# Gram products in eight row and column groups of TensorE, two batches at a time

## The chip, the cores and the metric

The kernel runs on one NeuronCore of a Trainium2 chip. The metric is device time in microseconds of one execution, the median over the runs shown. A profile page and a trace come from one more execution, which has a time of its own.

## What is computed

Inputs are q, k, v of shape (4 batches, 8 heads, 768 positions, 48) and beta of shape (4, 8, 768), with the weights of two layers that follow. The reference runs a delta rule per batch and head, and then two dense layers with a nonlinearity each:

```python
k_n = k / (np.linalg.norm(k, axis=-1, keepdims=True) + 1e-06)
for t in range(S):
    y[:, :, t] = np.einsum('bhd,bhde->bhe', q[:, :, t], state)
    v_old = np.einsum('bhde,bhd->bhe', state, kt)
    state = state + bt[:, :, :, None] * np.einsum('bhd,bhe->bhde', kt, vt - v_old)
# x: y as (3072 tokens, 384)
h = x @ w_in          # 384 -> 2048
g = np.where(h > 0.0, h, np.exp(np.minimum(h, 0.0)) - 1.0)
x = g @ w_out         # 2048 -> 384
# second layer: the same shapes, g = P(h) / Q(h), a cubic over a quadratic in |h|
```

All inputs are float32. The result is the second layer's output, 3072 x 384.

## The kernel before

**The delta rule by chunks.** The 768 positions are cut into 12 segments `s` of 64, and each segment of a head into two blocks of 32. For every segment, batch and pair of heads the kernel needs the Gram products of the 64 keys with the 64 keys and the 64 queries. From the key part it builds and inverts a 32 x 32 triangular system per block (the "T pieces", on DVE), and from the query part, masked, it gets the output. A segment has 4 batches x 4 head pairs = 16 units of two heads.

**A Gram item** (`g_item`, L268 to 288) before the change handles one batch of one segment: four head pairs, one matmul each at L279. The stationary operand is a 96 x 128 block-diagonal copy of k that the host lays out (two heads of 48 rows; 2 blocks x 2 heads x 32 columns), the moving operand is the 96 x 128 array of k and q (64 + 64 columns). The result, 128 x 128 per head pair, lands in one PSUM tile `gp` of the pool `pa`, which has three buffers. Then DVE multiplies the query half by a mask into `p` (L282), and ACT copies three pieces of the key half into `gd` (L286, L287) and `lo` (L288). Batches 2 and 3 have the halves of the 128 partitions exchanged, so that two batches lie beside each other in later matmuls.

**The loads of g_in** are issued by the SP queue from `gin_ahead` (L225, L238): one load brings two head pairs, 96 partitions x 512 floats, 192 KB. The first 28 loads but one go to places that are free at the start (`gin_park`, L207: the tile wo1, later x tiles), the others to a pool of two buffers `gin`. An item needs two loads, and after each of its halves one more load is issued. In `start` (L766) the order on SP is two loads, the mask, 15 loads, beta, the head mask.

**Around it.** Two segments form a window `w`, six windows in all. A list of events with due times in units of a slot (16 slots to a window) gives each piece of work its place, and a list scheduler orders the instructions of each engine from there, as data and buffers come free in its own estimate. Each engine runs its list in order. Within window w run the first layer's matmuls (`H` at L578 to 580, `O` at L596 to 598, 18 matmuls of 512 columns for each of 16 steps f), the chain of segment matmuls for window w+1 (`chain`), the T pieces for w+2 (L297, the transpose of `gd`, to L372), and the Gram items for windows 2 and on, eight a window: those of window w+2 are due from slot 8 to slot 15 before window w starts. Window 0 and 1 have their Gram items in the prologue, before the first layer runs. Weights are converted in the same time (`conv_*`, loads at L142 by SP).

The chain's pieces for a segment are `ks` (L449, four column groups of 32), `u1` (L460), `lo` (L471) and `u2` (L483), which work in two row halves with a PSUM tile `cb` for each half of the batches, then `yy` (L498, L505), `xx` (L517) and `ku` (L528). All their PSUM tiles come from `pa`: one for each `ks`, `y`, `xt` and `ku`, two for the `cb` pair from u1 until u2 is evacuated at L488. The chain of a window ends in `xs`, which `split_x` (L396, L397) splits for the next window. After the sixth window the second layer runs (L578 to 580 into h_a and h_b, L733), which holds no Gram work.

```python
ps = pa.tile([128, 4, 128], F32, tag="pa", name="gp")
for p2 in range(2):
    t, n = gin_t.pop((s, b, p2))
    for i in range(2):
        mm(out=ps[:, 2 * p2 + i], lhsT=t[:, i, 0:128], rhs=t[:, i, 128:256], start=True, stop=True)
    gin_l[0] -= n
    gin_ahead(1)
```

A float32 matmul shows as two matmul records and two weight-load records in the trace, called passes here.

Of the kernel before, what the change touches and what calls it, by code (L numbers as in the profile page):

```python
# [7 lines left out]
F32 = mybir.dt.float32  # L8
# [29 lines left out]
def kernel(  # L38
# [162 lines left out]
    gin_q = [(w, j, s, b, p2) for w in range(NW) for j, s in enumerate(WINS[w]) for b in range(4) for p2 in range(2)]  # L201
# [5 lines left out]
    def gin_park(i):  # L207
        if i < 12:
            return wo1.rearrange("p f n -> p (f n)")[0:96, 512 * i:512 * i + 512]
        if i < 15:  # L210
            if i == 12:
                xg["s"] = ap1.tile([128, 3, 512], F32, tag="xs", name="xg")
            return xg["s"][0:96, i - 12]
        if 16 <= i < 22:
            tag = "xh" if i < 19 else "xl"
            if i % 3 == 1:
                xg[tag] = mp.tile([128, 3, 512], F32R, tag=tag, name="xg", bufs=1)
            return xg[tag][0:96, (i - 16) % 3].bitcast(F32)
        if 22 <= i < 24:
            return mp.tile([128, 512], F32, tag="e", name="xg")[0:96]  # L220
        if 24 <= i < 28:
            return mp.tile([128, 512], F32R, tag="gh" if i < 26 else "gl", name="xg")[0:96].bitcast(F32)
        return None

    def gin_ahead(n):  # L225
        for _ in range(n):
            i = gin_n[0]
            if i == len(gin_q):
                return
            park = i < 15 or 16 <= i < 28  # L230
            if park or gin_l[0] < 2:
                w, j, s, b, p2 = gin_q[i]
                if park:
                    t = gin_park(i).rearrange("p (a b) -> p a b", b=256)
                else:
                    t = ap2.tile([96, 2, 256], F32, tag="gin", name="gin")
                    gin_l[0] += 1
                nc.sync.dma_start(out=t, in_=g_in[s, b, :, 2 * p2:2 * p2 + 2])  # L238
                gin_t[s, b, p2] = t, not park
                gin_n[0] += 1  # L240
# [27 lines left out]
    def g_item(j, s, b):  # L268
        u0 = 16 * j + 4 * b
        if b == 0:  # L270
# [3 lines left out]
        v0 = 4 * b  # L274
        ps = pa.tile([128, 4, 128], F32, tag="pa", name="gp")
        for p2 in range(2):
            t, n = gin_t.pop((s, b, p2))
            for i in range(2):
                mm(out=ps[:, 2 * p2 + i], lhsT=t[:, i, 0:128], rhs=t[:, i, 128:256], start=True, stop=True)  # L279
            gin_l[0] -= n  # L280
            gin_ahead(1)
        nc.vector.tensor_tensor(  # L282
            out=p_t[:, v0:v0 + 4], in0=ps[:, :, 64:128],
            in1=mp_sb[b // 2].unsqueeze(1).to_broadcast([128, 4, 64]), op=ALU.mult)
        b0, b1 = halves(b // 2)
        act(out=gd[b0, u0:u0 + 4], in_=ps[b0, :, 0:32], func=AF.Copy)  # L286
        act(out=gd[b1, u0:u0 + 4], in_=ps[b1, :, 32:64], func=AF.Copy)  # L287
        act(out=lo_t[b0, v0 % 8:v0 % 8 + 4], in_=ps[b0, :, 32:64], func=AF.Copy)  # L288
# [113 lines left out]
    def chain(w, slots=SLOTS):  # L402
# [8 lines left out]
        for j, s in enumerate(WINS[w]):  # L411
# [24 lines left out]
            def ks(hf, s=s, st=st):  # L436
# [8 lines left out]
                for u in range(8):  # L445
                    for n in range(4):
                        blk, h = divmod(n, 2)
                        o, i0 = 64 * (blk ^ hf) + 32 * h, 64 - 64 * (u // 4) + 32 * blk
                        mm(out=ps[o:o + 32, u], lhsT=kq[:, u, i0:i0 + 32], rhs=s_bd[:, 8 * hf + u, h], start=True, stop=True)  # L449
# [29 lines left out]
            def u2(j=j, st=st):  # L479
# [4 lines left out]
                for d in st:  # L484
                    ub = ap2.tile([128, 8, 2, D], F32, tag="ub", name="ub")
                    d["ub"] = ub
                    for h in range(2):
                        act(out=ub[:, :, h], in_=d["cb"], func=AF.Copy, scale=mh_sb[:, h:h + 1])  # L488
                    if w == 0:
                        warm(d["R"][:, 0, 0:16], Q[f"wd{j}"])  # L490
# [68 lines left out]
    def g_list(w):  # L559
        return [(lambda j=j, s=s, b=b: g_item(j, s, b)) for j, s in enumerate(WINS[w]) for b in range(4)]  # L560
# [205 lines left out]
    def start():  # L766
# [5 lines left out]
        gin_ahead(NV)  # L772
# [142 lines left out]
def layout(q, k, v, beta, moe_w_in, moe_w_out, moe2_w_in, moe2_w_out, moe2_a, moe2_b):  # L915
# [14 lines left out]
    ktbd = np.zeros((NSC, B, 96, 4, 2, 2, 32), f32)  # L930
    for h in range(2):
        ktbd[:, :, 48 * h:48 * h + 48, :, :, h, :] = kf[:, :, 48 * h:48 * h + 48].reshape(NSC, B, 48, 4, 2, 32)
    ktbd[:, 2:] = ktbd[:, 2:, :, :, ::-1].copy()
    ktbd = ktbd.reshape(NSC, B, 96, 4, 128)
    g_in = np.concatenate([ktbd, kf, qf], axis=-1)
# [9 lines left out]
    kv[:, 2:] = np.concatenate([kv[:, 2:, 64:], kv[:, 2:, :64]], axis=2)  # L945
# [50 lines left out]
```

## Time and profile before

| | |
|---|---|
| median of 3 runs | 1138.27 us (1136.64 to 1140.21) |
| profiled execution, its own time | 1129.3 us |
| its span | 1127.5 us |
| PE (TensorE) busy | 1037.9 us, 92% of the span |
| PE weight loads | 835.8 us, 74% |
| DVE (VectorE) | 904.5 us, 80% |
| ACT (ScalarE) | 771.7 us, 68% |
| POOL (GpSimd) | 466.4 us, 41% |
| mean granted TensorE clock | 0.954 of full speed |
| DMA, mean over the span | 81 GB/s |

Busy time of PE is not PE at its peak, since matmuls are pipelined: a matmul's duration reaches past the start of the next one, and the pace is read from starts. Windows of the first layer begin, by the split of x, at 109, 235, 353, 462, 561 and 649 us; the second layer follows from about 737 us. The first Gram matmul starts at 3.2 us, the last at 460.1.

### The profile page before, as it was taken

To read this page: it belongs to the slowest core of one execution; us is meant where nothing else is said; L and a number is where in the kernel's file an instruction comes from. 1 tells how busy PE (TensorE), PEld (TensorE's weight loads), DVE (VectorE), ACT (ScalarE), POOL (GpSimd) and SP (SyncE) were. 2 spreads that over 40 slices of the span, in tenths; PEclk is the share of its full clock that TensorE was granted. 3 is DMA by queue.
4 is the path that set the end of the run, shared out by engine and by line. 5 is a ranking of instruction groups with operands and counts; after the bars stand their busy time and mean duration, and the time that the engine had idled before them with its cause. 6 is when DMAs were issued, how large, how long until landed. Compare 5 with 4: busy or idle time off the path is not lost.

```text
span 1127.5 us, 20636 instructions
## 1 busy us (share of the span) xinstructions
PE 1037.9 (92%) x7952; PEld 835.8 (74%) x7952; DVE 904.5 (80%) x1240; ACT 771.7 (68%) x1525; POOL 466.4 (41%) x399
## 2 busy tenths in 40 slices
PE   7178898889798999899999999999999999999997
PEld 7155676667676778777888878778788888888885
DVE  4989889689857873795434379999999999999997
ACT  5568687866577546665665689976767667676764
POOL 1376655434332322242332145446363544536342
PEclk8559899999899989998999999999999999999999
DMA  9436343454364113120212044400100001010000
GB/s 287 155 102 200 116 147 114 131 161 126 97 189 149 59 50 121 60 81 1 81 49 62 1 148 133 120 28 1 56 1 25 32 1 56 1 56 1 29 1 28
DMA packets 51842, 91.75 MB, mean 81 GB/s; under 512 B 7072, under 2 KB 29728, under 8 KB 51744
## 3 DMA queue, kind: packets, MB, share of 16 engines
q1 hardware_dynamic: 51744, 90.43, 25.8%
q8 instruction: 62, 1.02, 0.4%
q14 instruction: 36, 0.29, 0.1%
HBM read 77.83 MB, written 12.58 MB: 80 GB/s over the span
## 4 chain that ended last, share of the span: by engine, by line
PE 54%; DVE 24%; ACT 7%; issue 6%; DMA 5%; POOL 3%; SPq 0%; ACTq 0%; DVEq 0%; POOLq 0%
PE o L733 13%; PE h_a L578 6%; PE h_a L579 6%; PE h_a L580 6%; DVE tmp L345 5%; PE o L596 3%; PE o L597 3%; PE o L598 3%; PE h_b L578 2%; PE h_b L579 2%; PE h_b L580 2%; DMA raw<-w_out 2%; DVE tt L346 2%; PE gp L279 2%; DVE wo L695 2%
## 5 line engine op out<-in xcount | busy, mean ns | idle before, releaser
L710 POOL TENSOR_TENSOR gl<-wo 128x1024 fp32r<-128x1024 f32 x47 | 147.3, 3134 | 202.4 <-DVE wo L709 174.2
L72 POOL TENSOR_TENSOR wor<-wo,wor 128x384 fp32r<-128x384 f32 x96 | 109.1, 1137 | 268.0 <-ACT wor L71 260.3
L578 PE MATMUL h_a<-xh,wi 128*128 128x512 f32 x417 | 173.9, 417 | 10.1 <-ACT pe L608 8.8
L579 PE MATMUL h_a<-xl,wi 128*128 128x512 f32 x417 | 168.9, 405 | 3.7 <-DVE xl L397 3.7
L580 PE MATMUL h_a<-xh,wi 128*128 128x512 f32 x417 | 167.8, 402 | 0.0
L733 PE MATMUL o<-gh,wo 128*128 128x512 f32 x564 | 135.9, 390 | 0.4 <-ACT ys L741 0.4
L613 DVE SCALAR_TENSOR_TENSOR e<-e,pe 128x512 f32<-128x512 f32 x96 | 70.8, 737 | 75.4 <-ACT e L609 75.1
L733 PEld LDWEIGHTS o<-gh,wo 128*128 128x128 f32 x564 | 105.2, 188 | 23.8 <-ACT ys L741 2.4
L596 PE MATMUL o<-gh,wor 128*128 128x512 f32 x288 | 115.8, 410 | 0.0
L597 PE MATMUL o<-gl,wor 128*128 128x512 f32 x288 | 114.5, 398 | 1.2 <-DVE gl L621 1.2
L598 PE MATMUL o<-gh,wor 128*128 128x512 f32 x288 | 113.0, 392 | 0.0
L578 PEld LDWEIGHTS h_a<-xh,wi 128*128 128x128 f32 x417 | 80.8, 194 | 30.5 <-ACT pe L608 10.9
L621 DVE TENSOR_TENSOR gl<-e,gh 128x512 fp32r<-128x512 f32 x88 | 79.2, 900 | 29.3 <-ACT gh L619 28.9
L579 PEld LDWEIGHTS h_a<-xl,wi 128*128 128x128 f32 x417 | 81.3, 195 | 22.1 <-DVE xl L397 7.2
L607 ACT ACTIVATE e<-h_a 128x512 f32<-128x512 f32 x91 | 54.2, 596 | 58.6 <-PE h_a L580 58.2
L580 PEld LDWEIGHTS h_a<-xh,wi 128*128 128x128 f32 x417 | 81.1, 194 | 17.3
L696 ACT ACTIVATE wo<-wo 128x1024 f32<-128x1024 f32 (+1 forms) x49 | 51.3, 1046 | 60.4 <-DVE wo L695 60.4
L619 ACT ACTIVATE gh<-e 128x512 fp32r<-128x512 f32 x96 | 60.0, 625 | 35.0 <-DVE e L613 35.0
L695 DVE SCALAR_TENSOR_TENSOR wo<-wo 128x1024 f32<-128x1024 f32 (+1 forms) x49 | 73.1, 1492 | 4.5 <-ACT wo L688 4.4
L71 ACT ACTIVATE wor<-wo 128x384 fp32r<-128x384 f32 x96 | 50.4, 525 | 35.7 <-PE o L598 35.3
L733 PE MATMUL o<-gl,wo 128*128 128x512 f32 x282 | 71.7, 389 | 0.8 <-POOL gl L710 0.8
L707 DVE SCALAR_TENSOR_TENSOR gh<-wo,ab_sb 128x1024 fp32r<-128x1024 f32 (+1 forms) x49 | 65.5, 1336 | 6.6 <-ACT wo L697 0.6
(168 smaller groups left out, 2462.8 us busy)
## 6 DMA issues: line engine op xcount, KB each, us to landing
kv<-c_kv SPq DMA_DIRECT2D x24, 576.0 KB, 4.6
gin<-g_in SPq DMA_DIRECT2D x69, 192.0 KB, 2.9
kq<-c_kq SPq DMA_DIRECT2D x22, 512.0 KB, 3.8
raw<-w_out SPq DMA_DIRECT2D x42, 192.0 KB, 2.5
raw<-w_in SPq DMA_DIRECT2D x34, 192.0 KB, 2.4
wo<-w_in SPq DMA_DIRECT2D x30, 192.0 KB, 2.7
xr<-x2d SPq DMA_DIRECT2D x6, 768.0 KB, 5.3
out_t<-ys SPq DMA_DIRECT2D x18, 256.0 KB, 2.2
```

What stands on the lines that cost most here:

```text
L72: eng.tensor_tensor(out=t[:, 1], in0=src, in1=t[:, 0].bitcast(F32), op=ALU.subtract)
L578: mm(out=ps, lhsT=hi, rhs=xh[:, c, 0:NC], start=(c == 0), stop=False)
L579: mm(out=ps, lhsT=hi, rhs=xl[:, c, 0:NC], start=False, stop=False)
L580: mm(out=ps, lhsT=lo, rhs=xh[:, c, 0:NC], start=False, stop=(c == 2))
L596: mm(out=ps[:, 0:NC], lhsT=hi[:, cs], rhs=gh[:, 0:NC], start=(f == 0), stop=False)
L597: mm(out=ps[:, 0:NC], lhsT=hi[:, cs], rhs=gl[:, 0:NC], start=False, stop=False)
L598: mm(out=ps[:, 0:NC], lhsT=lo[:, cs], rhs=gh[:, 0:NC], start=False, stop=(f == NF - 1))
L613: nc.vector.scalar_tensor_tensor(out=e, in0=e, scalar=-1.0, in1=p, op0=ALU.add, op1=ALU.add)
L621: eng.tensor_tensor(out=gl[:, 0:NC], in0=e, in1=gh[:, 0:NC].bitcast(F32), op=ALU.subtract)
L695: v.scalar_tensor_tensor(out=sq, in0=sq, scalar=1.0 + 1e-6, in1=ab, op0=ALU.add, op1=ALU.add)
L710: (v if k == NK - 1 else nc.gpsimd).tensor_tensor(out=gl, in0=sq, in1=ab, op=ALU.mult)
L733: mm(out=ps, lhsT=wo2[2 * j + i][:, int(p == 1), cs], rhs=(gl if p == 2 else gh)[:, n], start=(j == 0 and p == 0 and i == 0), stop=(j == N ...
```

## The change

The block-diagonal copy of k is left out of g_in: a load is now 128 partitions (two heads, each 48 rows and 16 rows of zeros) x 2 head pairs x 128 floats (k and q), 128 KB. An item now handles two batches, c and c+2, and half of their head pairs (part 0 or 1); there are again eight items a window. It needs two loads, one for each batch. For each head pair it issues eight matmuls of 48 rows, 32 stationary columns and 128 moving columns: two blocks x two heads x two batches, each in another pair of row half and column group. Two PSUM tiles, one per batch, are taken in part 0 and evacuated after part 1. The heads within the second pair of batches change places, which the layout of kv and beta and the mask of ub follow. The loads of windows 0 and 1 (32 of them) all go to parked places and are issued at the start, ahead of beta and the head mask; later loads have six buffers, and three are asked for after each item.

```diff
-    gin_q = [(w, j, s, b, p2) for w in range(NW) for j, s in enumerate(WINS[w]) for b in range(4) for p2 in range(2)]
+    gin_q = [(s, b, p) for w in range(NW) for s in WINS[w] for c in range(2) for p in range(2) for b in (c, c + 2)]
...
+        n = slice(256 * (i % 2), 256 * (i % 2) + 256)
+        if i < 16:
+            return wo1.rearrange("p f n -> p (f n)")[:, 256 * i:256 * i + 256]
+        i = i // 2 - 8
+        tag = ("xs", "xh", "xl")[i // 3]
...
-            park = i < 15 or 16 <= i < 28
-            if park or gin_l[0] < 2:
-                w, j, s, b, p2 = gin_q[i]
+            park = i < 32
+            if park or gin_l[0] < 6:
+                s, b, p = gin_q[i]
...
-                    t = ap2.tile([96, 2, 256], F32, tag="gin", name="gin")
+                    t = ap2.tile([128, 2, 128], F32, tag="gin", name="gin", bufs=6)
...
-    def g_item(j, s, b):
...
-        ps = pa.tile([128, 4, 128], F32, tag="pa", name="gp")
-        for p2 in range(2):
-            t, n = gin_t.pop((s, b, p2))
-            for i in range(2):
-                mm(out=ps[:, 2 * p2 + i], lhsT=t[:, i, 0:128], rhs=t[:, i, 128:256], start=True, stop=True)
-            gin_l[0] -= n
-            gin_ahead(1)
-        nc.vector.tensor_tensor(
-            out=p_t[:, v0:v0 + 4], in0=ps[:, :, 64:128],
-            in1=mp_sb[b // 2].unsqueeze(1).to_broadcast([128, 4, 64]), op=ALU.mult)
-        b0, b1 = halves(b // 2)
-        act(out=gd[b0, u0:u0 + 4], in_=ps[b0, :, 0:32], func=AF.Copy)
-        act(out=gd[b1, u0:u0 + 4], in_=ps[b1, :, 32:64], func=AF.Copy)
-        act(out=lo_t[b0, v0 % 8:v0 % 8 + 4], in_=ps[b0, :, 32:64], func=AF.Copy)
+    def g_item(j, s, c, part):
...
+        if part == 0:
+            gp_t[0] = [pa.tile([128, 4, 128], F32, tag="pa", name="gp") for _ in range(2)]
+        tp = [gin_t.pop((s, c + 2 * hf, part)) for hf in range(2)]
+        for i in range(2):
+            u = 2 * part + i
+            for blk in range(2):
+                for h in range(2):
+                    for hf in range(2):
+                        t = tp[hf][0]
+                        rs = slice(64 * h, 64 * h + D)
+                        o = 64 * (blk ^ hf) + 32 * (h ^ hf)
+                        mm(out=gp_t[0][hf][o:o + 32, u], lhsT=t[rs, i, 32 * blk:32 * blk + 32], rhs=t[rs, i], start=True, stop=True)
+        gin_l[0] -= sum(t[1] for t in tp)
+        gin_ahead(3)
+        if part == 0:
+            return
+        for hf in range(2):
+            b = c + 2 * hf
+            ps = gp_t[0][hf]
+            u0, v0 = 16 * j + 4 * b, 4 * b
+            nc.vector.tensor_tensor(
+                out=p_t[:, v0:v0 + 4], in0=ps[:, :, 64:128],
+                in1=mp_sb[hf].unsqueeze(1).to_broadcast([128, 4, 64]), op=ALU.mult)
+            b0, b1 = halves(hf)
+            act(out=gd[b0, u0:u0 + 4], in_=ps[b0, :, 0:32], func=AF.Copy)
+            act(out=gd[b1, u0:u0 + 4], in_=ps[b1, :, 32:64], func=AF.Copy)
+            act(out=lo_t[b0, v0 % 8:v0 % 8 + 4], in_=ps[b0, :, 32:64], func=AF.Copy)
...
-                        o, i0 = 64 * (blk ^ hf) + 32 * h, 64 - 64 * (u // 4) + 32 * blk
+                        o, i0 = 64 * (blk ^ hf) + 32 * (h ^ hf), 64 - 64 * (u // 4) + 32 * blk
...
-                        act(out=ub[:, :, h], in_=d["cb"], func=AF.Copy, scale=mh_sb[:, h:h + 1])
+                        act(out=ub[:, :, h], in_=d["cb"], func=AF.Copy, scale=mh_sb[:, h ^ hf:(h ^ hf) + 1])
...
-        return [(lambda j=j, s=s, b=b: g_item(j, s, b)) for j, s in enumerate(WINS[w]) for b in range(4)]
+        return [(lambda a=(j, s, c, part): g_item(*a)) for j, s in enumerate(WINS[w]) for c in range(2) for part in range(2)]
...
-        gin_ahead(NV)
+        gin_ahead(30)
...
+    g_in = np.zeros((NSC, B, 2, 64, 4, 128), f32)
+    g_in[:, :, :, :Dh] = np.concatenate([kf, qf], axis=-1).reshape(NSC, B, 2, Dh, 4, 128)
...
-    kv[:, 2:] = np.concatenate([kv[:, 2:, 64:], kv[:, 2:, :64]], axis=2)
+    kv[:, 2:] = np.concatenate([kv[:, 2:, 32 * i:32 * i + 32] for i in (3, 2, 1, 0)], axis=2)
...
-            beta_l[w, :, 16 * j + 8:16 * j + 16] = bt[s][[2, 3, 0, 1], 8:16]
+            beta_l[w, :, 16 * j + 8:16 * j + 16] = bt[s][::-1, 8:16]
```

## Rows read from the trace of the kernel before

**Rows 1.** Three windows of the first layer: stretch, length, busy us (instructions), clock, DMA, GB/s.
```profile
109.00:237.00 128.00, 111.69 (x1108) 88.25 (x1109) 105.95 (x188) 97.87 (x269) 65.95 (x78) 0.96 0.46 141
355.00:464.00 109.00, 103.42 (x1071) 83.68 (x1070) 73.14 (x126) 65.54 (x143) 29.85 (x30) 0.95 0.23 75
464.00:561.00 97.00, 92.12 (x998) 73.36 (x997) 66.62 (x114) 56.66 (x114) 31.48 (x28) 0.96 0.17 56
```

**Rows 2.** Chain that ended last, from 0 to 66 us: start, us, what.
```profile
3.06 4.59 DMA wo<-g_in
...
7.70 8.74 PE gp L279 x48
...
17.57 1.96 DVE am L297
```

**Rows 3.** Timeline of PE at a Gram item: start, us, engine, line, form, count.
```profile
350.54 1.05 PE L279 MATMUL gp<-gin 96*128 96x128 f32 x8
351.35 0.48 PE L596 MATMUL o<-gh,wor 128*128 128x512 f32 x1
351.67 0.40 PE L597 MATMUL o<-gl,wor 128*128 128x512 f32 x1
351.90 0.39 PE L598 MATMUL o<-gh,wor 128*128 128x512 f32 x1
```

**Rows 4.** Timeline of PE at a pair of ks, four column groups.
```profile
289.77 0.39 PE L598 MATMUL o<-gh,wor 128*128 128x512 f32 x1
290.09 1.59 PE L449 MATMUL ks<-s_bd,kq 128*32 128x48 f32 x128
291.61 0.50 PE L578 MATMUL h_a<-xh,wi 128*128 128x512 f32 x1
```

**Rows 5.** Groups by line, ks: count, busy us, mean ns, idle before, releaser.
```profile
L449 PE MATMUL ks<-s_bd,kq 128*32 128x48 f32 x1408 | 18.1, 207 | 1.9 <-issue 1.9
```

**Rows 6.** Timeline of PE at cb (L471), two row halves with a column half each.
```profile
256.20 1.14 PE L471 MATMUL cb<-R,lb 64*64 64x48 f32 x32
257.27 0.50 PE L578 MATMUL h_a<-xh,wi 128*128 128x512 f32 x1
```

**Rows 7.** Two stretches of the start, as rows 1: 96-partition, then 128-partition loads.
```profile
8.00:10.00 2.00, 2.00 (x11) 2.00 (x11) 0.19 (x1) 0.76 (x3) 0.00 (x0) 1.00 1.01 294
26.00:28.00 2.00, 1.72 (x8) 1.72 (x9) 1.79 (x9) 1.54 (x7) 0.00 (x0) 0.50 1.03 416
```

**Rows 8.** Timeline of the SP queue at the start.
```profile
0.74 0.87 SPq L238 DMA_DIRECT2D wo<-g_in  x2
...
2.12 4.79 SPq L238 DMA_DIRECT2D wo<-g_in  x10
```

**Rows 9.** Timeline of all engines at the start.
```profile
3.21 4.24 PE L279 MATMUL gp<-wo 96*128 96x128 f32 x16 [3.21 <-DMA wo<-g_in]
...
5.32 0.42 DVE L282 TENSOR_TENSOR p<-gp,cm_sb 128x256 f32<-128x256 f32 x1 [5.32 <-PE gp L279]
5.84 0.27 ACT L286 ACTIVATE gd<-gp 64x128 f32<-64x128 f32 x1 [3.83 <-DVE p L282]
...
7.70 6.94 PE L279 MATMUL gp<-wo 96*128 96x128 f32 x32 [0.25 <-DMA wo<-g_in]
...
22.99 0.19 DVE L321 TENSOR_TENSOR x<-x,bl 128x32 f32<-128x32 f32 x1
```

**Rows 10.** Tile gin, who waited for it: us, times.
```profile
  PE gp L279: 6.3, 7
```

**Rows 11.** Waits of the SP queue over the span: us, times, longest.
```profile
SPq L238 <- PE gp L279: 50.0, 31, 12.6
```

**Rows 12.** Timeline of PE: item 0 of window 5, u1, item 1.
```profile
408.28 1.05 PE L279 MATMUL gp<-gin 96*128 96x128 f32 x8
...
413.10 0.31 PE L460 MATMUL cb<-R,tb 64*64 64x48 f32 x2 [1.70 <-DVE R L452]
...
419.44 1.52 PE L279 MATMUL gp<-gin 96*128 96x128 f32 x8
```

More of the change, by code (lines that the diff above doesn't have):

```diff
@@ L207, in gin_park @@
     def gin_park(i):
[L208 to L223, printed above, removed]
+        n = slice(256 * (i % 2), 256 * (i % 2) + 256)
[3 more added lines that the diff above has]
+        tag = ("xs", "xh", "xl")[i // 3]
+        if tag not in xg:
+            pool, dt = (ap1, F32) if tag == "xs" else (mp, F32R)
+            xg[tag] = pool.tile([128, 3, 512], dt, tag=tag, name="xg", bufs=1)
+        t = xg[tag][:, i % 3, n]
+        return t if tag == "xs" else t.bitcast(F32)
     def gin_ahead(n):
@@ L229, in gin_ahead @@
                 return
-            park = i < 15 or 16 <= i < 28
-            if park or gin_l[0] < 2:
-                w, j, s, b, p2 = gin_q[i]
+            park = i < 32
+            if park or gin_l[0] < 6:
+                s, b, p = gin_q[i]
                 if park:
-                    t = gin_park(i).rearrange("p (a b) -> p a b", b=256)
+                    t = gin_park(i).rearrange("p (a b) -> p a b", b=128)
                 else:
-                    t = ap2.tile([96, 2, 256], F32, tag="gin", name="gin")
+                    t = ap2.tile([128, 2, 128], F32, tag="gin", name="gin", bufs=6)
                     gin_l[0] += 1
-                nc.sync.dma_start(out=t, in_=g_in[s, b, :, 2 * p2:2 * p2 + 2])
-                gin_t[s, b, p2] = t, not park
+                nc.sync.dma_start(out=t, in_=g_in[s, b, :, 2 * p:2 * p + 2])
+                gin_t[s, b, p] = t, not park
                 gin_n[0] += 1
@@ L266, in halves @@
         return (slice(64 * hf, 64 * hf + 64), slice(64 - 64 * hf, 128 - 64 * hf))
-    def g_item(j, s, b):
-        u0 = 16 * j + 4 * b
-        if b == 0:
+    gp_t = {}
+    def g_item(j, s, c, part):
+        if (c, part) == (0, 0):
             p_d[s] = ap2.tile([128, 16, 64], F32, tag="p", name="p", bufs=4)
@@ L273, in g_item @@
         p_t, lo_t = p_d[s], lo_d[s]
-        v0 = 4 * b
-        ps = pa.tile([128, 4, 128], F32, tag="pa", name="gp")
-        for p2 in range(2):
-            t, n = gin_t.pop((s, b, p2))
-            for i in range(2):
-                mm(out=ps[:, 2 * p2 + i], lhsT=t[:, i, 0:128], rhs=t[:, i, 128:256], start=True, stop=True)
-            gin_l[0] -= n
-            gin_ahead(1)
-        nc.vector.tensor_tensor(
-            out=p_t[:, v0:v0 + 4], in0=ps[:, :, 64:128],
-            in1=mp_sb[b // 2].unsqueeze(1).to_broadcast([128, 4, 64]), op=ALU.mult)
-        b0, b1 = halves(b // 2)
-        act(out=gd[b0, u0:u0 + 4], in_=ps[b0, :, 0:32], func=AF.Copy)
-        act(out=gd[b1, u0:u0 + 4], in_=ps[b1, :, 32:64], func=AF.Copy)
-        act(out=lo_t[b0, v0 % 8:v0 % 8 + 4], in_=ps[b0, :, 32:64], func=AF.Copy)
+        if part == 0:
[25 more added lines that the diff above has]
+            act(out=lo_t[b0, v0 % 8:v0 % 8 + 4], in_=ps[b0, :, 32:64], func=AF.Copy)
     def t_pieces(w):
@@ L483, in u2 @@
                         mm(out=d["cb"][b1, u], lhsT=d["tb"][b1, u].rearrange("p a b -> p (a b)"), rhs=d["R"][b1, u], start=True, stop=True)
-                for d in st:
+                for hf, d in enumerate(st):
                     ub = ap2.tile([128, 8, 2, D], F32, tag="ub", name="ub")
@@ L929, in layout @@
     kf, qf = feat(k), feat(q)
[L930 to L935, printed above, removed]
+    g_in = np.zeros((NSC, B, 2, 64, 4, 128), f32)
+    g_in[:, :, :, :Dh] = np.concatenate([kf, qf], axis=-1).reshape(NSC, B, 2, Dh, 4, 128)
+    g_in = g_in.reshape(NSC, B, 128, 4, 128)
     kq = np.stack([np.concatenate([qf, kf] if b % 2 == 0 else [kf, qf], axis=-1)[:, b] for b in range(B)], axis=1)
```

## The prediction, made before the changed kernel was timed

> **What bounds the kernel now.** I read the stretches of the first layer first, each from one split of x to the next, then the PE rows inside them, then the chain that ended last. In the window that begins at 355 us PE is busy for 103.4 of 109.0 us, DVE for 73.1, ACT for 65.5; the window at 464, which holds no Gram item but a like load otherwise, takes 97.0 [rows 1]. So PE is close to being the bound there, and 12 us separate a window with eight Gram items from one without. The window at 109, which holds the items of two windows, is not PE's: PE 111.7 of 128.0, DVE 105.9. The start is another matter: the chain goes from a landing of g_in (issued at 3.06, there at 7.65) through 48 Gram passes to the transpose of gd at 17.57 [rows 2], the first step of window 0's work on DVE. Gram work is therefore on the path at the start, nearly on it in some windows, and absent after 461 us. The second half of the run isn't touched.
>
> A Gram item before is four matmuls, each of two passes in the trace (fp32), so 8 passes. At the full clock the item holds PE from 350.54 to 351.35, 0.81 us or 101 ns a pass, and the next matmul but one starts 0.32 later where 0.23 is usual, 0.09 for leaving: 0.90 in all [rows 3].
>
> **The change part by part.**
>
> *The Gram passes.* An item becomes 16 matmuls of 48 rows by 32 weight columns, 32 passes, with the same 128 moving columns. If nothing overlapped, an item would cost 32 x 101 ns = 3.2 us; everything hangs on how many of the eight groups run side by side. No row shows eight. The nearest for column groups is ks: four of them, 48 moving columns, 128 passes from 290.09 to 291.61, 11.9 ns each [rows 4]. A single 48-column pass by the Gram rate is 101 x 48/128 = 38 ns, so four groups give 38/11.9 = 3.2, 80% of perfect. The nearest for row groups is cb, whose consecutive matmuls differ in row half and column half: 32 passes in 1.07 us, 33.4 ns each, only 38/33.4 = 1.14 times better than no overlap [rows 6]. Its weights are 64 columns wide, though, against 32 in ks and here; at the Gram rate 64 columns of either operand are 50 ns, and two groups side by side can then do no better than 25. So the shortfall can be weight width rather than row halves. Ends: eight groups, perfect, 12.6 ns a pass, 0.40 us an item; four groups at ks's 80%, 101/3.2 = 31.6 ns, 1.01 us. I take eight at 80%, 15.8 ns and 0.51 us, because in width and number of groups the item is nearest to ks. Going from full-array matmuls to grouped ones costs 290.09 - 289.77 - 0.23 = 0.09 [rows 4], and I let leaving cost 0.09 as now. New item 0.69, saving 0.21; ends 0.58 (saving 0.32) and 1.19 (loss 0.29).
>
> The Trainium skill (TensorE: Matmul & The Clock Gate, Measured speedup vs the span model) gives 6.32 times for nine row-and-column groups; an estimate by that page, 5.6 for eight, makes 18 ns a pass, 0.58 us and with the crossings 0.76, so that the saving would be 0.14 and the sum 1.3 us worse. No row here shows it.
>
> 32 items run at the full clock (for windows 2 to 5): 6.7 us of PE. How much reaches the end? By the 12 us between two windows, of which eight items are 7.2, nearly all where PE is at 95%, little in the window at 109, which holds half of them. I take 0.6: **-4** (ends -6 and +6).
>
> *The issue of them.* 576 more matmuls, each with its weight load. ks, which issues as densely, lost 1.9 us to issue over 1408 passes [rows 5]; the new kernel has 1536 Gram passes in smaller bursts. Bound 0 to 2; I take 0, since an item is a quarter of a ks burst and the next item stands some us away.
>
> *The start.* Before, loads of 192 KB over 96 partitions come at 294 GB/s, and 128-partition transfers later reach 416 [rows 7]. Sixteen loads and the 128 KB mask are 3.3 MB, about 11 us after 2 us. PE then works at 217 ns a pass (32 passes in 6.94 us, half the clock, though the clock column prints 1.00) and is what ends the stage [rows 7, 9]. After, a load is 128 KB, so SP is the limit: ten issues take 4.79 us [rows 8]. Seventeen issues at 0.45 from 0.74 end at 8.4; the first load is there for PE at 3.21, 2.5 behind its issue [rows 8, 9], so the last data is there at 10.9, or at 13.0 if a landing takes 4.59 as in [rows 2]; I take 10.9, as 128 KB in 0.45 us is 291 GB/s, well under 416, and nothing then piles up. A part at half clock takes 2 x 0.51 = 1.0, close to the pace of two loads, so the last ends at 12.0. The evacuation of a pair is then one DVE multiply and five ACT copies before gd is whole: 5.84 - 5.32 = 0.52, plus 5 x 0.285 (a copy takes 0.27 and its successor starts 0.28 to 0.29 behind it), 1.95 [rows 9]. The transpose starts at 14.0, not 17.57: **-3.6**. Ends: -3.8 with perfect groups; with four groups a part is 2.0, eight parts from 3.2 end at 19.4, transpose at 21.3, +3.8. The new order puts beta and the head mask behind 33 issues, not 18: issued at 15.6, landed by 18, needed first by the multiply with beta, 22.99 - 17.57 = 5.4 us behind the transpose's start [rows 2, 9], at 19.4. Cover is 1.4 us; each us that they land later than that is lost from the 3.6. kq, kv and the first weights stand behind the same number of g_in loads as before, each a third smaller, so they're no later than now. All of window 0's DVE work follows the transpose, so I let the gain reach the end of the prologue.
>
> *The loads in the windows.* Two buffers of one item become six of half an item (half an item of one batch pair needs two loads). PE sat idle before Gram matmuls for 6.3 us waiting for g_in [rows 10]. SP itself stood 50.0 us behind those buffers [rows 11], with weight, kq and kv loads queued behind it; deeper buffers shorten that too. Issue count stays 96. I take half of 6.3, since after such a wait other matmuls were late as well: **-3** (ends -6.3 and 0).
>
> *The PSUM pair.* Two of the three pa tiles are now held from part 0 until part 1 is evacuated, and u1 needs two, every y, xt and ku one. Item 0 of window 5 is at 408.28, u1 at 413.10, item 1 at 419.44 [rows 12]: u1 must move behind item 1 and its evacuation, some 9 us, with lo, u2 and y behind it on PE and DVE. Other matmuls fill PE meanwhile, if they stand ahead. An evacuation to the last copy is 0.52 + 6 x 0.285 = 2.2 us; 16 pairs are 35 us, the upper end, 0 the lower. I take +2.5, since o matmuls stand directly behind the Gram item of [rows 3].
>
> The evacuations themselves are the same number and shape. New positions of parked loads, the reversed heads in kv and beta and the other mask column for ub change no instruction: 0, with nothing that they need to hide behind.
>
> **Sum:** -4 - 3.6 - 3 + 2.5 = -8.1 against the profiled execution's 1129.3 (span 1127.5), so 1121.2. That execution lies 9.0 under the median shown, 1138.27; taking the same 8.1 off the median gives **1130**. Own range 1124 to 1135.
>
> **Rivals.**
>
> *Groups share no column (the change doesn't do what it says).* Only the four column groups overlap; the two row halves take turns. For it: cb's 1.14. Against it: cb's wide weights. Start +3.8, items 32 x 0.29 x 0.6 = +5.6, loads -3, PSUM +2.5: +8.9, **1147**. It decides as soon as a pass takes over 22 ns, where an item stops being cheaper. The Trainium skill (TensorEngine Tiling (Array Packing), Gotcha 1: PSUM Pressure) says that different row tiles can't use one PSUM bank at the same time; here both row halves write both tiles, on different partitions, and no row of before has that. By that rule this rival is the outcome.
>
> *PE waits for the pair's evacuation.* Place: the first user of pa behind each part 1, u1 above all. If half of the 35 us stands open on PE: -3.6 - 4 - 3 + 17.6 = +7.0, **1145**. It decides from about 10.6 us of open waits. For it: u1 comes between two parts in each later window [rows 12]. Against: h and o matmuls lie between.
>
> *Gains off the path.* DVE and ACT set the windows; only the start and the PSUM wait count: -1.1, **1137**.
>
> *All of it lands:* every item, every load wait, no PSUM cost: -3.6 - 6.7 - 6.3 = -16.6, **1122**.
>
> **How the numbers follow.** Forecast 0.45, all lands 0.10, off the path 0.17, PSUM wait 0.15, no column shared 0.13. A measurement of this kernel can tell 0.3%, 3.4 us: under 1134.9 is faster, over 1141.7 slower. Faster: 0.45 + 0.10 + a little of the off-path case = 0.57; same: the rest of it and the mild end of the PSUM wait, 0.18; slower 0.25. The range reaches from the case where all lands to just short of the one without shared columns, 1122 to 1146; half of each lies outside, about 0.12.
>
> **What would show it.** In the changed profile: Gram passes of about 16 ns, 0.5 us an item at the full clock (30 ns would mean four groups); the first transpose near 14 us, and the last of the prologue earlier by as much; PE's wait for g_in near zero; u1 behind Gram part 1. Wrong would be: windows at 237 and 355 no shorter than 118 and 109 us, PE idle behind gd or lo copies before cb, y or ku, or a multiply with beta that waits for its DMA.

## The result, and the profile after

The changed kernel takes 1147.67 us (median of 8 runs, 1142.17 to 1149.04), the kernel before on the same chip 1138.29 (8 runs): ratio 1.0096, 95% interval 1.0070 to 1.0122. It is slower by about 9 us, clear of the noise. The prediction said 1130 and 1122 to 1146.

The profiled execution took 1147.5 us (span 1145.7). The one of before took 1129.3, 9 us under its median, so the two traces differ by twice what the medians do; a second profile of before, below, shows where. Line numbers after: Gram matmul L280, p L289, gd and lo L293 to L295, transpose of gd L304, R L459, ks L456, u1 L467, split of x L403, o L603 to L605.

Three windows of the changed kernel, columns as in [rows 1], and two stretches of 4 us inside the second:

```profile
118.20:244.20 126.00, 109.92 (x1454) 82.29 (x1454) 104.88 (x187) 92.06 (x252) 61.19 (x70) 0.92 0.42 128
364.60:477.40 112.80, 104.78 (x1262) 80.17 (x1261) 72.30 (x124) 64.71 (x140) 31.64 (x30) 0.94 0.18 60
477.40:578.00 100.60, 94.79 (x1002) 75.59 (x1001) 67.68 (x114) 58.26 (x117) 33.49 (x28) 0.95 0.17 54
424.00:428.00 4.00, 2.71 (x34) 2.04 (x35) 2.27 (x4) 0.83 (x2) 0.20 (x2) 0.50 0.14 35
428.00:432.00 4.00, 4.00 (x24) 2.86 (x24) 0.03 (x1) 1.10 (x3) 0.50 (x1) 0.70 0.12 37
```

The first window begins 9 us later than before (118.2, not 109), and the one with eight Gram items lasts 112.8 us, not 109 [rows 1]. In it PE is idle for 8.0 us where it was for 5.6. PE's longest waits of Gram and ks matmuls over the whole span (who waited for whom, us, times, longest), and its one wait of u1 for a copy of the pair:

```profile
PE gp L280 <- DVE R L459: 7.8, 2, 4.2
PE ks L456 <- DVE R L459: 7.0, 1, 7.0
PE gp L280 <- ACT lo L295: 4.1, 6, 1.7
PE gp L280 <- DMA wo<-g_in: 2.9, 1, 2.9
PE cb L467 <- ACT lo L295: 0.4, 1, 0.4
```

The 6.3 us for later loads of g_in [rows 10] are gone. In their place are 14.8 us in three waits for R, the subtraction on DVE that empties a PSUM tile of ks; before had no such wait of a Gram or ks matmul (u1 waits for R in both). The first, on the timeline of PE:

```profile
188.44 0.89 PE L456 MATMUL ks<-s_bd,kq 128*32 128x48 f32 x64
189.25 0.67 PE L280 MATMUL gp<-gin 48*32 48x128 f32 x32
189.85 0.50 PE L603 MATMUL o<-gh,wor 128*128 128x512 f32 x1
197.39 1.51 PE L456 MATMUL ks<-s_bd,kq 128*32 128x48 f32 x64 [7.04 <-DVE R L459]
198.83 0.80 PE L604 MATMUL o<-gl,wor 128*128 128x512 f32 x1
199.42 0.63 PE L605 MATMUL o<-gh,wor 128*128 128x512 f32 x1
```

DVE in the same time:

```profile
189.46 1.52 DVE L620 SCALAR_TENSOR_TENSOR e<-e,pe 128x512 f32<-128x512 f32 x1
...
191.24 1.49 DVE L352 TENSOR_TENSOR tmp<-xx_t,tt 128x768 f32<-128x768 f32 x1
...
194.83 1.92 DVE L352 TENSOR_TENSOR tmp<-xx_t,tt 128x1024 f32<-128x1024 f32 x1
196.78 0.55 DVE L459 TENSOR_TENSOR R<-kv,ks 128x384 f32<-128x384 f32 x1
197.25 0.75 DVE L289 TENSOR_TENSOR p<-gp,cm_sb 128x256 f32<-128x256 f32 x2
```

The Gram pair holds two of the three tiles of `pa`, the first half of ks has the third, and the second half of ks stands until one is empty. ks ends at 189.3, but R comes at 196.78: DVE runs its list in order, and T pieces, e and weight conversions stand ahead. The pair's own p stands behind R. At 310 and 425 the same happens the other way round: the two halves of ks have two tiles, the pair's part 0 takes the last for its first matmul (2 passes), and its second tile waits for R:

```profile
416.94 1.58 PE L456 MATMUL ks<-s_bd,kq 128*32 128x48 f32 x128
...
420.72 0.40 PE L280 MATMUL gp<-gin 48*32 48x128 f32 x2
425.29 1.10 PE L280 MATMUL gp<-gin 48*32 48x128 f32 x30 [4.16 <-DVE R L459]
426.31 0.79 PE L603 MATMUL o<-gh,wor 128*128 128x512 f32 x1
426.91 0.63 PE L604 MATMUL o<-gl,wor 128*128 128x512 f32 x1
...
429.89 0.63 PE L605 MATMUL o<-gh,wor 128*128 128x512 f32 x1
```

Behind each of the three the granted clock falls to the lower of its two levels, 1.2 GHz (0.50 in 424 to 428, above): o matmuls start 0.43 us apart instead of 0.23, nine of them here, and the Gram part takes 1.02 instead of 0.60. That is 2.2 us on top of 4.16.

A Gram part at the full clock, to set beside [rows 3]:

```profile
356.33 0.67 PE L280 MATMUL gp<-gin 48*32 48x128 f32 x32
356.93 0.50 PE L603 MATMUL o<-gh,wor 128*128 128x512 f32 x1
357.26 0.40 PE L604 MATMUL o<-gl,wor 128*128 128x512 f32 x1
```

32 passes in 0.60 us, 18.75 ns each, 0.10 more for leaving (0.33 where 0.23 is usual); with the prediction's 0.09 for entering, 0.79. And the start, PE, DVE and ACT in order, beside [rows 2, 9]:

```profile
9.51 0.76 DVE L289 TENSOR_TENSOR p<-gp,cm_sb 128x256 f32<-128x256 f32 x2 [2.71 <-PE gp L280]
9.96 0.27 ACT L293 ACTIVATE gd<-gp 64x128 f32<-64x128 f32 x1 [1.68 <-DVE p L289]
...
10.53 0.27 ACT L295 ACTIVATE lo<-gp 64x128 f32<-64x128 f32 x1
...
10.85 3.07 PE L280 MATMUL gp<-wo 48*32 48x128 f32 x64 [0.27 <-ACT lo L295]
...
18.23 1.97 DVE L304 STREAM_TRANSPOSE am<-gd 128x1024 f32<-128x1024 f32 x1 [1.22 <-ACT gd L294]
```

The pairs take turns with their evacuation, and the first transpose starts at 18.23 (before 17.57, forecast 14.0). SP's waits behind the buffers of g_in grew from 50.0 us [rows 11] to 65.5:

```profile
SPq L232 <- PE gp L280: 65.5, 25, 17.8
```

### The profile page after: what moved, and what is told of

Its sections match the earlier page's. It is cut to its first block, busy times and chain, and to the rows that moved or that the text cites. A ratio compares the mean times of both kernels' runs of the same rounds, so it can differ in the third digit from the quotient of the medians.

```text
span 1145.7 us, 22987 instructions
## 1 busy us (share of the span) xinstructions
PE 1039.4 (91%) x9104; PEld 819.0 (71%) x9104; DVE 905.9 (79%) x1240; ACT 772.1 (67%) x1525; POOL 472.4 (41%) x399
## 4 chain that ended last, share of the span: by engine, by line
PE 58%; DVE 21%; ACT 8%; issue 5%; DMA 3%; POOL 3%; SPq 0%; ACTq 0%; DVEq 0%; POOLq 0%
PE o L740 13%; PE h_a L585 6%; PE h_a L587 6%; PE h_a L586 6%; DVE tmp L352 5%; PE o L603 3%; PE o L604 3%; PE o L605 3%; PE gp L280 2%; PE h_b L585 2%; PE h_b L586 2%; PE h_b L587 2%; DVE tt L353 2%; DMA raw<-w_out 2%; PE cb L467 2%
## 5 line engine op out<-in xcount | busy, mean ns | idle before, releaser
L603 PE MATMUL o<-gh,wor 128*128 128x512 f32 x288 | 118.4, 419 | 0.0
L604 PE MATMUL o<-gl,wor 128*128 128x512 f32 x288 | 116.4, 404 | 1.2 <-DVE gl L628 1.2
L605 PE MATMUL o<-gh,wor 128*128 128x512 f32 x288 | 115.2, 400 | 0.2 <-POOL wor L72 0.2
L714 DVE SCALAR_TENSOR_TENSOR gh<-wo,ab_sb 128x1024 fp32r<-128x1024 f32 (+1 forms) x49 | 65.5, 1337 | 7.5 <-ACT wo L704 1.5
```

Of the source, the lines that this page charges most:

```text
L603: mm(out=ps[:, 0:NC], lhsT=hi[:, cs], rhs=gh[:, 0:NC], start=(f == 0), stop=False)
L604: mm(out=ps[:, 0:NC], lhsT=hi[:, cs], rhs=gl[:, 0:NC], start=False, stop=False)
L605: mm(out=ps[:, 0:NC], lhsT=lo[:, cs], rhs=gh[:, 0:NC], start=False, stop=(f == NF - 1))
```

## The experiments

The edits are against the changed kernel unless said otherwise. "Ratio" is to the kernel before on the same chip, with its 95% interval. "R waits" are PE's waits of Gram and ks matmuls for R. "Split" is where the split of x of window 0 starts, read off ACT's timeline; the last column has the lengths of the four windows from there, each from one split to the next. All but the first three columns are from one profiled execution each.

| run | median us | ratio | R waits us | transpose | split | windows 0 to 3 |
|---|---|---|---|---|---|---|
| before | 1138.3 | | 0 | 17.57 | 108.9 | 126.3, 118.1, 108.8, 98.7 |
| before, again | 1139.3 (one run) | | 0 | 16.65 | 113.5 | 131.1, 119.6, 107.7, 99.0 |
| changed | 1147.7 | 1.0096 (1.0070, 1.0122) | 14.8 | 18.23 | 118.2 | 126.0, 120.4, 112.9, 100.6 |
| changed, again | 1145.3 | 1.0073 (1.0037, 1.0109) | 14.8 | 19.15 | 117.9 | 127.2, 115.4, 110.2, 100.4 |
| one batch | 1123.7 | 0.9882 (0.9829, 0.9934) | 0 | 15.28 | 111.6 | 121.4, 115.7, 105.5, 99.7 |
| merged parts | 1138.7 | 1.0021 (0.9988, 1.0053) | 4.7 | 18.69 | 119.3 | 123.8, 121.8, 107.3, 99.8 |
| other banks | 1143.3 | 1.0045 (1.0015, 1.0076) | 14.2 | 15.42 | 119.8 | 124.2, 120.5, 112.6, 100.4 |
| beta first | 1142.0 | 1.0034 (1.0006, 1.0062) | 13.7 | 18.68 | 116.6 | 125.2, 120.9, 112.6, 100.4 |
| in turns | 1142.9 | 1.0058 (1.0024, 1.0091) | 14.2 | 16.95 | 116.4 | 127.8, 119.7, 112.3, 100.5 |
| four groups first | 1140.2 | 1.0029 (0.9999, 1.0059) | 11.9 | 15.71 | 113.1 | 124.9, 117.1, 111.1, 97.2 |
| late evacuation | 1121.3 | 0.9887 (0.9851, 0.9922) | 0 | 15.58 | 113.0 | 119.0, 116.0, 105.5, 99.8 |
| two tiles, four groups | 1151.3 | 1.0131 (1.0081, 1.0181) | 13.6 | 20.68 | 122.4 | 126.6, 116.9, 111.3, 98.8 |

**Again: both kernels once more.**

> The changed kernel once more, beside the others on one chip, to see which stage times repeat between two profiled executions. All theories: 1144 to 1150, first transpose at 18 to 18.5, split of x of window 0 at 117.5 to 119, and waits of Gram and ks matmuls for R near 310, 425 and 197 us in the same places; stage times that move by more than 1 us are those that a single profile can't carry.

> The kernel before once more, for a second profile, as its first one (1129.3 us) lies 9 us under its median. All theories: 1130 to 1141. If the prologue repeats as it did in the changed kernel (118.2 and 117.9), the split of x is at 108.5 to 110 and the 9 us between the kernels there are real; a split at 112 or later would make half of them an accident of the first profile. What the time is above 1129 must then be found in the windows from 109 to 462 us, at 1.2 GHz.

The three R waits of the changed kernel repeat to 0.1 us (7.04, 3.55 and 4.20, after 7.04, 3.64 and 4.16), and its split to 0.3; its transpose moved by 0.9, to 19.15. The window at 244 does not repeat: 120.4 and 115.4 us, at a mean clock of 0.94 and 0.99. In before the split itself moved, 108.9 to 113.5, so half of the 9 us that the prologue seems to lose is an accident of the first profile, as one expectation had allowed. A stage difference of under 5 us in two single profiles says little here.

**One batch per item, one tile.**

```diff
-    def g_item(j, s, c, part):
+    def g_item(j, s, b):
...
-            gp_t[0] = [pa.tile([128, 4, 128], F32, tag="pa", name="gp") for _ in range(2)]
+        ps = pa.tile([128, 4, 128], F32, tag="pa", name="gp")
...
+        for u in range(4):
+            t, i = tp[u // 2][0], u % 2
```

> An item again holds one batch and one PSUM tile, as before the change, but keeps the new loads and the 48-row products: 16 matmuls in four column groups. Theory PSUM pair: the time is lost where the second tile of a pair waits for the evacuation of ks's or of the last pair's tile. Then PE's wait of Gram matmuls for ACT and DVE, about 22 us on this pool in the changed kernel, falls to 3 to 6 us, the first transpose comes at 16 to 18 us, and the time falls to 1138 to 1142 although a pass is dearer (four groups: 27 to 31 ns, 32 x 0.3 us = 9.6 us more PE in the windows, 0.6 of it open). Theory prologue order: the pieces of window 0 still lie between weight conversions, the split of x stays within 2 us of 118, and the time stays at 1147 or rises to 1153 by the dearer passes. Theory loads: the time follows the number of g_in loads issued at the start, unchanged here, so 1147 to 1153 as well.

1123.7: 24 us under the changed kernel and 13 under the one before, more than any theory asked. No wait for R is left, and a part takes 1.01 us (31.5 ns a pass) where it took 0.60. So the Gram passes got dearer and the kernel faster.

**Parts merged.**

```diff
+        def pair(j, s, c, part):
+            if part == 1:
+                g_item(j, s, c, 0)
+                g_item(j, s, c, 1)
...
```

> Both parts of a pair are issued together where part 1 stood, so the two PSUM tiles are held for 1.2 us and the evacuation, not from part 0 on. Theory PSUM pair: the waits of Gram matmuls and ks for R (7.8 and 7.0 us) go or halve, and 4 to 8 us come back: 1140 to 1144; the start is unchanged, with the first transpose at 18 to 18.5, as there the pairs follow each other without a gap in any case. Theory prologue order: no more than 2 us, 1146 to 1149, with the split of x near 118 us. If the two-part item is what fills PE well between other work, a merged one costs and the time rises.

1138.7: with the pair held for a short time only, one R wait (4.73 us) is left of three, and 7 to 9 us come back. The prologue stays as it was, as expected. The two waits that went were not gained whole: the window at 243, which lost one of 3.6 us, is no shorter (121.8 us). PE waits there 8.6 us for ACT to empty tiles of h_a, where it waited 4.5 in the changed kernel.

**Other banks at the start.**

```diff
+            if s < 4 and c == 1:
+                gp_t[0] = [po.tile([128, 512], F32, tag=f"o{i}", name="gp").rearrange("p (a b) -> p a b", b=128) for i in (1, 2)]
```

> In the prologue alone the second pair of each scan step takes two banks of the output pool, unused then, instead of the common one. Theory PSUM pair: at the start the third and fourth pair stop waiting for ACT's copies, and the first transpose comes 2 to 4 us earlier, at 14.2 to 16.2; the split of x comes earlier by as much and the time falls to 1143.5 to 1145.5. Theory prologue order: the first transpose may come earlier, but the split of x stays near 118 (within 1.5 us) and the time at 1147, because what lies between 18 and 68 us is an interleaving with weight conversions that moves with it.

The transpose came 2.8 us earlier, so the turns at the start are a matter of tiles; the split came no earlier, and 2 to 4 us in the time are within the scatter. What the start gains is lost again before the split; which step loses it stays open.

**Beta first.**

```diff
-        gin_ahead(30)
+        gin_ahead(14)
         load_beta(0)
         nc.sync.dma_start(out=mh_sb, in_=mask_h)
+        gin_ahead(16)
```

> At the start only window 0's 16 loads of g_in are issued first; beta and the head mask come next and the loads of window 1 behind them. Theory loads: beta, mask, kq and the first weights reach the chip late behind 32 loads; with 16 of them moved back, beta lands some 8 us earlier, and the pieces of window 0 after the transpose get shorter by 3 to 6 us: the split of x at 112 to 115 and the time 1142 to 1145. Theories PSUM pair and prologue order: beta isn't waited for, the split of x stays within 1 us of 118, the time at 1146 to 1149, first transpose at 18 to 18.5.

Split 1.6 us earlier, time 3 us under the second measurement of the changed kernel: between the theories, at the edge of what can be told. The same edit on the one-batch kernel gave nothing:

> One batch per item, and at the start beta and the head mask ahead of window 1's loads. In the changed kernel this order took the split from 118 to 116.6 and the time from 1145.3 to 1142.0. If the two add up: split at 110, time at 1120 to 1122. If what the order gave was the wait of window 1's Gram products behind the pair, nothing is left to gain and it stays at 1123 to 1125.

It measured 1124.7 (ratio 0.9913, 0.9882 to 0.9945).

**The kernel before with three buffers; one batch with four half buffers.** The first edit is against the kernel before.

```diff
-            if park or gin_l[0] < 2:
+            if park or gin_l[0] < 3:
...
-            gin_ahead(1)
+            gin_ahead(2)
```

> The kernel before, with its block-diagonal copy and full-array products, and only a third buffer for g_in (as much room as the changed kernel takes). Theory loads: the gain of the run with one batch per item over the kernel before comes from loads that are there in time; PE's 6.3 us of waits for g_in fall under 2.5, and with them go the stretches at 1.2 GHz that follow the waits at 136.8 and 340.7 us (1.6 and 2.5 us long): 1126 to 1131. Theory smaller products: the waits go but the time stays at 1134 to 1138, since the gain comes from the start and from the weight loads that stood behind g_in on SP.

```diff
-            if park or gin_l[0] < 6:
+            if park or gin_l[0] < 4:
...
```

> One batch per item with four buffers of half an item for g_in, the room that the kernel before had, where there were six. Theory loads: the gain over the kernel before (13 us) comes from loads issued further ahead; with four, waits of Gram matmuls for g_in come back to 5 to 8 us and the time to 1129 to 1135. Theory smaller loads: 128 KB over 128 partitions instead of 192 KB over 96 are there in time with four buffers as well: waits under 3 us, 1123 to 1126.

Before with a third buffer: 1133.8, ratio 0.9991 (0.9957 to 1.0025), no change. PE's waits for g_in did not go (16.8 us; 18.5 in the second profile of before, against 6.3 in its first), so the run says nothing on what early loads are worth. The one-batch kernel with four half buffers instead of six: 1131.4, ratio 0.9983 (0.9950 to 1.0017), some 8 us given back. But its trace has only one wait of PE matmuls for these loads, 1.6 us, so the price of depth is shown and its path is not.

**The changed kernel with four**, by the same edit.

> The changed kernel with four buffers of half an item for g_in instead of six, the room that the kernel before took. With one batch per item this took 1123.7 to 1131.4 us. If the depth of the loads is worth as much here, 1150 to 1155, with PE waits for g_in back at 3 to 8 us. If the waits for PSUM cover the loads (what would come late for a Gram product that stands anyway costs nothing), 1143 to 1148.

1143.3, ratio 1.0050 (1.0018 to 1.0082): the depth is worth nothing where the R waits stand (14 us of them remain).

**The start by hand.** On the one-batch kernel, everything due before -48.5 keeps the program's order.

```diff
-    ma=-200, xo=2.244,
+    ma=-48.5, xo=2.244,
...
```

> One batch per item, and the instructions of the start in the order in which the program emits them, where the scheduler had ordered them before: 13 instead of 16 weight conversions then stand on DVE ahead of tp_t (11 in the kernel before, 17 in the changed one). Theory prologue order: tp_t starts at 61 to 62.5 instead of 64.2, the split of x 2 to 3 us earlier than 111.6, the time 1120.5 to 1122. Theory chain behind: the chain from tp_t to the split sets it (47 us in each kernel), conversions that are done later stand in its way, and the split stays within 1 us and the time at 1123 to 1125.

1129.3, ratio 0.9920 (0.9892 to 0.9949), and tp_t at 65.3: a miss. DVE stood 2.8 us for beta and 2.2 for gd. With 10 to 18 conversions ahead of tp_t, the way from the transpose of gd to the split took 96 to 102 us in 15 of the 17 profiles (96.3 with one batch, 96.8 in before's second profile, 99.9 in the changed one; 91.3 in before's first, 104.4 with other banks). The number of conversions doesn't order these, so nothing here shows that it sets the time.

**In turns; four groups first.** The first edit, then the second; in both the order of the loops over blk, h, i and hf changes and nothing else:

```diff
-            for blk in range(2):
-                for h in range(2):
-                    for hf in range(2):
+            for hf in range(2):
+                for blk in range(2):
+                    for h in range(2):
```
```diff
-        for i in range(2):
+        for hf in range(2):
...
+            for i in range(2):
...
```

> The changed kernel with its pair of batches, two PSUM tiles and all waits, but the eight matmuls of a pass group issued batch by batch, so that only four column groups stand side by side, as in the run with one batch per item (31 ns a pass there, 1123.7 us). Theory PSUM pair: holding two tiles is what costs, so the waits stay and dearer passes come on top: 32 parts by 32 passes by 12.5 ns are 12.8 us of PE, 0.6 of it open, 1152 to 1157. Theory eight groups: something in running eight groups (row halves of two tiles alternating) is what costs, and in turns they give the time back: 1124 to 1132. Between these, 1146 to 1150, PE time in Gram passes isn't on the path at all.

> The pair with both PSUM tiles held from part 0 on, as in the changed kernel, but in each part first all eight matmuls of one batch, then all eight of the other, so that only four column groups work side by side and a pass takes 31 ns, as in the runs that hold one tile or none (1121.3, 1123.7 us). Theory two tiles held: the waits for R stay (7.0, 3.6 and 4.2 us near 197, 307 and 420 us) and the time is that of the changed kernel, 1145, plus 32 parts by 32 passes by 12.5 ns, half to all of it in the open: 1146 to 1155. Theory eight groups: the loss comes from running eight groups together, and with four the time falls to 1121 to 1128 although two tiles are held.

Both failed in what they meant to do. In the first a part still takes 0.60 us; in the second most parts take 0.6 to 0.7. Issued in another order, the two batches still lie in eight different groups, and overlap. In the second run some parts were split by the scheduler: one batch's 16 passes alone take 0.57 us (35.6 ns each), both batches' 32 take 0.62:

```profile
432.25 0.64 PE L280 MATMUL gp<-gin 48*32 48x128 f32 x16
432.82 1.14 PE L490 MATMUL cb<-R,tb 64*64 64x48 f32 x32
...
440.71 0.69 PE L280 MATMUL gp<-gin 48*32 48x128 f32 x32
441.33 0.50 PE L585 MATMUL h_a<-xh,wi 128*128 128x512 f32 x1
```

So 1142.9, and 1140.2 with ratio 1.0029 (0.9999 to 1.0059), both with R waits, tell nothing on four groups against eight. The second tells something else: its split comes as early as with one tile held (113.1), and its R waits stand (11.9 us).

**Late evacuation: one tile held.** Part 0 computes the first batch whole, part 1 the second, and both are evacuated behind part 1.

```diff
-            gp_t[0] = [pa.tile([128, 4, 128], F32, tag="pa", name="gp") for _ in range(2)]
+            gp_t[0] = []
+        gp_t[0].append(pa.tile([128, 4, 128], F32, tag="pa", name="gp"))
...
```

> The passes of the run with one batch per item (four groups, the loads batch by batch), but the first batch of a pair keeps its PSUM tile until the second batch is computed, and both are evacuated together, as in the changed kernel: one tile is held from part 0 on, where the changed kernel holds two and the run with one batch per item none. Theory PSUM pair: the cost is by the tiles held. With two of three tiles left, ks and the next Gram part needn't wait for R, so the three waits of 7.0, 3.6 and 4.2 us near 197, 307 and 420 go, and the time lies between 1124 and 1145, at 1127 to 1134. Rival, the bunch: the cost is in evacuating two tiles in a row (six copies on ACT, two multiplies on DVE) where other work waits on these engines: 1140 to 1146, with waits on ACT's lo or DVE's p in place of those on R.

1121.3, as fast as the run that holds none and faster than the 1127 to 1134 expected, though it evacuates in the same bunch. The rival, the bunch, falls. Its waits of Gram and ks matmuls longer than 1 us, and the place where the changed kernel waits 7.04 us; here the two halves of ks run on without a break, with the Gram part right behind:

```profile
PE gp L280 <- DMA wo<-g_in: 3.6, 2, 3.0
PE gp L280 <- DMA gin<-g_in: 2.9, 2, 1.7
PE gp L280 <- ACT lo L295: 2.8, 2, 2.1
PE ks L456 <- issue: 1.4, 1, 1.4
```
```profile
182.54 1.58 PE L456 MATMUL ks<-s_bd,kq 128*32 128x48 f32 x128
184.05 1.08 PE L280 MATMUL gp<-gin 48*32 48x128 f32 x32
```

**Two tiles, four groups.** Only the rows of the second batch change places, so the pair meets itself in the same four groups.

```diff
-                        rs = slice(64 * h, 64 * h + D)
+                        rs = slice(64 * (h ^ hf), 64 * (h ^ hf) + D)
...
+    g_in[:, 2:] = g_in[:, 2:, ::-1].copy()
```

> The pair with both PSUM tiles held from part 0 on, and the changed kernel's order of passes, but the heads of the second batch lie in the other row half of g_in (its rows are stored the other way round), so that the two batches meet in the same four row and column groups instead of in eight. Theory two tiles held: the waits for R stay (7.0, 3.6 and 4.2 us), a pass takes 31 ns instead of 18.75, and the time is 1145 to 1155. Theory eight groups: with four groups the time falls to 1121 to 1128 although two tiles are held. If a pass stays near 19 ns, the pace isn't set by the number of groups.

1151.3. The waits are those of the changed kernel, and a part is as dear as with one tile (1.01 us from its first pass to the next matmul):

```profile
346.27 1.08 PE L280 MATMUL gp<-gin 48*32 48x128 f32 x32
347.28 0.50 PE L585 MATMUL h_a<-xh,wi 128*128 128x512 f32 x1
```
```profile
PE gp L280 <- DVE R L459: 7.1, 2, 4.1
PE ks L456 <- DVE R L459: 6.5, 1, 6.5
```

This settles the main point. At the same pace of passes, holding two tiles instead of one (the order of the loads within a pair differs too) is worth 1.0131 - 0.9887 = 2.4%, 28 us; by the two intervals, 21 to 35. Of the 23 us between the two profiles, 9 lie before the split and 14 in the three windows that hold a wait for R. Four groups first, whose split is as early as late evacuation's (113.1 and 113.0), is 12.6 us longer in these three windows and has 11.9 us of R waits: the waits cost without the late start as well.

With two tiles held, eight groups instead of four are worth 1.0131 less 1.0096 or 1.0073, 4 to 7 us, which these intervals can't tell from nothing. All that the change brings besides (loads, smaller products) is worth 1.1%, 13 us, by the late evacuation against before. These three differences add up to the changed kernel's +9 by construction, so their sum is no check on them.

Not tried were a fourth buffer of `pa` and an R that stands earlier in DVE's list. The list scheduler also orders each of these kernels anew, so a part of any difference may be its order.

Late evacuation and one batch per item beat the kernel before by 1.1 to 1.2%, and the changed one by about 2%.

## Why the prediction was wrong

**The step that failed is the PSUM pair**, put at +2.5 us and measured at about 28 (21 to 35) with four groups; the changed kernel itself lies 1.9 to 2.1%, 21 to 24 us, above late evacuation. It was sized by how long the evacuation of a pair takes (2.2 us, 16 times), and the prediction asked who waits behind the pair. What costs is that a pair needs two free tiles of three while ks has two of its own, and that whoever comes second waits for R. How late R is does not come from the pair's evacuation: DVE has up to 7 us of other work ahead of it. The rows for it were there: a pair of ks, one tile each, runs without a break [rows 4], DVE is busy for 105.95 of 128 us in the first window [rows 1], and a wait for R already stood ahead of u1 [rows 12]. The rival "PE waits for the pair's evacuation" had the cause nearly right (1145, chance 0.15) and the place wrong: u1 waited 0.4 us for the pair in the whole run. The three waits with the slow matmuls behind them are some 20 us (14.8, and 1.5 to 2.2 at 1.2 GHz behind each). The profiles of the changed kernel and of late evacuation differ by 26 us: 5 before the split (118.2 against 113.0), 19 in the three windows with the waits (7.0, 4.4 and 7.4), the rest after them. That these 19 are the waits is the natural reading, but in the second profile of the changed kernel they are 12 with the same waits, and merged parts did not get two such waits back whole.

The Trainium skill (Perfetto Trace Analysis, Optimization Strategy) says that the same gap coming back on the engine that should be saturated can mean too little PSUM for the next tile. The three gaps here, one in each of three windows (7.04, 3.64 and 4.16 us), agree with that.

**Gram passes**, -4: the direction was right for PE's time in an item. A pass takes 18.75 ns, not 15.8, and an item 0.79, not 0.69; the saving is 0.11 and not 0.21, half the term. The estimate from the Trainium skill (TensorE: Matmul & The Clock Gate, Measured speedup vs the span model), 18 ns, was nearer. What the eight are worth in the end against four groups (31.5 ns), 4 to 7 us, is not clear of the noise.

**Groups share no column** (1147, 0.13): the number was met, the mechanism not. The passes overlap across row halves, and kernels with the pace of this rival are the fastest of all. The Trainium skill (TensorEngine Tiling (Array Packing), Gotcha 1: PSUM Pressure) has different row tiles kept from one PSUM bank at a time. Here both row halves write both tiles, on other partitions, and the trace doesn't bear that out. If only one row half at a time could write a tile, at most four of the eight groups could work at once, by estimate 25 ns a pass from the 101 of [rows 3]; 18.75 was measured, and 31.5 in the run whose two batches share four groups.

**The start**, -3.6: not there. The transpose is at 18.2 (19.2 in the second profile), not 14.0. A part takes about 1.5 us there (64 passes in 3.07), where the sum had 1.0, and PE waits for the pair's last copy before each next pair. With at most one tile held from one part to the next the transpose is at 14.1 to 15.6 (five profiles), so the waits for the pair cost the term some 3 us. In four groups first, whose parts begin with eight matmuls into one tile alone, it is at 15.71, which fits: what costs there is that the first matmuls of a part need both tiles. "All of window 0's DVE work follows the transpose, so I let the gain reach the end of the prologue" failed too: 2.8 us won there by other banks did not reach the split.

**Loads**, -3: PE's waits for them went, as said. SP's own waits behind the buffers did not get shorter, as the prediction had it, but grew to 65.5 us. What the depth is worth is 8 us with one tile and nothing measurable with two, presumably since the R waits cover it.

**The range** ended at 1146, just short of the case without shared columns (1147, half of which it left out); 1147.67 lies past it. Besides the pair the sum had -10.6. Late evacuation lies 13 us under before, but at the pace of four groups, without the start's -3.6 and with half of the Gram term gone, so that this agreement is in part luck.

## What to carry to other kernels

Two tiles taken at once from a pool of three are priced by who else takes two, and by how deep the queue is that empties theirs, not by how long one's own evacuation takes. Before pairing work for more overlap on TensorE, ask for each pool which tiles are held when the second is asked for; if the partner can come later, as in the late evacuation, take its tile later. An engine that gets its products cheaper gains little where it then stands 15 us for room to put them.

## What was unexpected of the hardware

Eight groups gave 18.75 ns a pass and four 31.5: 1.7 times, not 2. The order in which the eight are issued made little difference (0.60 us a part in the changed kernel and in turns, 0.6 to 0.7 with four groups first). After each R wait of 3.6 to 7 us the matmuls of the changed kernel ran at the pace of 1.2 GHz, for some 4 to 5 us in its first profile and 3 in its second, so that a wait cost 1.3 to 2.2 us more than itself. And runs of one kernel spread over 7 to 17 us (before: 1128.2 to 1145.0 in 29 runs). Where such stretches at 1.2 GHz fall has a part in it: the same window of the changed kernel took 120.4 us at a mean clock of 0.94, and 115.4 at 0.99.
